# Order of ScalarE's work behind transform groups, and the steps in which first-stage groups run

## The chip, the cores and the metric

The kernel runs on one core of a Trainium2 chip. The metric is the device time of one execution in microseconds; lower is better. TensorE (PE) multiplies matrices and accumulates in PSUM banks of 128 partitions by 512 floats; VectorE (DVE), ScalarE (ACT) and GpSimd (POOL) work on elements; SyncE (SP) mostly issues DMAs. Each engine works through its own queue of instructions in the order in which the kernel wrote them.

## What is computed

The input x is 8 batches of 3008 tokens of 256 floats. First a Fourier transform along the tokens and one along the 256 features, of which the real part is kept; then a two-layer block with the quick gelu:

```
X = np.fft.fft(np.fft.fft(x, axis=1), axis=2).real.astype(np.float32)
h = X.reshape(24064, 256) @ w_in          # 256 x 2048
g = h * (1.0 / (1.0 + np.exp(-1.702 * h)))
out = g @ w_out                            # 2048 x 256
```

## The kernel before

**The transform.** The transform along the 3008 tokens is split as 47 by 64. For the next batch, b + 1, it is made while batch b goes through the two layers. `load_x` (L199) brings the batch to `xt` in SBUF, in four pieces; `fold1` (L210) adds and subtracts mirrored features on POOL, in 8 pairs of parts; `mix1` (L233) is the first stage: four groups of matmuls (m = 0 to 3) for each batch, each into two PSUM banks, `ps[0]` and `ps[1]`, that two ScalarE copies (L258) bring back to `xt`. Of the two copies, number r takes bank `ps[r]`. `spill` (L332) writes a finished group to DRAM (`Td`), and `fill` (L337) reads it back in another layout. `rotate` (L342) is a small correction of one column, and `stage2` (L349) is the second stage: 64 matmuls into two banks, and four DVE transposes of them to `pq`. The feature transform is folded into the first layer's weights (`wcs`). `paced` is a tiny DMA that holds back the DMAs behind it on SP's queue until a step's result is there.

**The steps.** The two layers run in 384 steps (L503): 8 batches x 3 blocks x 2 halves x 8 pairs of hidden groups. Step t makes two hidden groups of 128 for 256 tokens and their mirror tokens; in the second half of a batch's first block (steps 8 to 15 of its 48) a step is 226 tokens wide (`width`, L511). From step 8 on, the work of a step is this:

- `middle(t)` (L580): two ScalarE activations (L587) that write the rank-one term (the row `nb` times a weight per partition) to x's PSUM bank, `b0` or `b1` by the step's parity.
- `begin(t)` and `begin(t, 1)` (L590): 8 TensorE instructions each that add the even and then the odd part of the transform to that bank (rows "x<-pq,wcs" of the profile). A step starts with `begin(t, 1)` and issues `begin(t + 1)` later on.
- `doubled(t)` (L596, L599): ScalarE copies the bank, doubled, after `begin(t)` and before `begin(t, 1)` may add to it.
- `forward(t)` (L601): the gelu of the sum. `backward(t)` (L604, L560): a DVE subtraction that gives the mirror tokens, and `activate_back` (L609) their gelu.
- `sums` (L617 on POOL, L624 and L625 on DVE) and `deeper` (L646, DVE): sums for the second layer, which is multiplied by a seven-product scheme, one quarter of it once more in seven smaller ones.
- `product(t - 3)` (rows "o<-big,wo"), 12 instructions for most steps, and `small_products` (rows "low<-big", "o<-big,wo" of L680) of steps t - 3 and t - 4: the second layer, three steps behind (`LAG`). After 8 steps of one half the results are combined (`combine`, `combine_small`, `swap`, `combine_last`) and stored.

**The order.** It is written out by hand: the loop at L984 issues each step's work, and a table `extra` adds transform work at the end of chosen steps (`at`, L928; the loop that fills it for all batches is at L953). In a step that ends with `mix1` or `stage2` (`special`, L1022), x's bank of that parity and `b2` are lent to it, and `middle(t + 2)` is left out; the next step (`after`) makes up for it with `middle(t + 1)` ahead of `begin(t + 1)`. In an `after` step more of the products is placed ahead of `begin(t + 1)`. The order also changes in a step where the product three steps behind opens a new accumulation:

```
opening = (t - LAG) % NP == 0 and t >= NP + LAG
...
cut = 0 if opening and not after else 3 if after else 2
product(t - LAG, 0, cut)
...
    begin(t + 1)
...
product(t - LAG, cut, 6 if t - LAG == last else None)
```

`stage2` ends steps 8, 24 and 40 of a batch. `mix1` ended steps 12, 15, 19 and 23 of batches 1 to 6, and 16, 20, 25 and 28 of batch 0 (the last batch has none). `spill` follows in the step behind each group.

Of the kernel before, what the change touches and what calls it, by code (L numbers as in the profile page):

```python
# [50 lines left out]
def free(ap, offset, *dims):  # L51
    return bass.AP(ap.tensor, ap.offset + offset, [list(ap.ap[0])] + [list(d) for d in dims])
# [60 lines left out]
def kernel(ctx: ExitStack, tc, x, w_in, w_out, tab1, tab2, out):  # L113
    nc = tc.nc
    B, S, D = x.shape
# [53 lines left out]
    def bank(name, tag=None):  # L169
        if tag is None:  # L170
            tag = spare.pop(0)
            spare.append(tag)
        if tag in ("o0", "o1"):
            return o_banks[int(tag[1])]
        return (rest if tag[0] == "o" else psp).tile([128, 512], F32, tag=tag, name=name)
# [11 lines left out]
    xt = xp.tile([128, NJ, D], F32, tag="x", name="xt")  # L187
# [45 lines left out]
    def mix1(b, m):  # L233

        ps = [bank("ps1") for _ in range(2)]
        queues = {}
        for i in (2 * m, 2 * m + 1):
            for r in range(2):
                for c in range(2):
                    rows, o = slice(64 * r, 64 * r + NA), ps[r][64 * c:64 * c + 64, i % 2 * D:(i % 2 + 1) * D]  # L240
                    jj, todo = 4 * i + 2 * r + c, queues.setdefault((r, c), [])
                    if jj:
                        todo.append((2, o, mat(w1, jj, rows), xt[rows, 31 - (2 * i + c), :], not todo, True))
                        continue
                    for k, c0, c1 in ((0, 0, H + 1), (1, H + 1, D)):
                        for part in range(2):
                            todo.append((1, o[:, c0:c1], mat(w1, ENDS[k + 2 * part], rows), e0[b][:, part, c0:c1], not todo,
                                         part == 1))

        had = {key: 0 for key in queues}  # L250
        while any(queues.values()):
            key = min((key for key in queues if queues[key]), key=lambda key: (had[key], key))
            size, o, w, rhs, first, end = queues[key].pop(0)
            had[key] += size
            nc.tensor.matmul(o, lhsT=w, rhs=rhs, start=first, stop=end, skip_group_check=True)  # L255

        for r in range(2):
            nc.scalar.copy(free(xt[:], (4 * m + r) * D, [2 * D, 2], [1, D]), free(ps[r][:], 0, [D, 2], [1, D]))  # L258

# [314 lines left out]
    def activate(t):  # L576
        g = free(ht[t][:], 0, [256, 4], [1, width(t)])
        nc.scalar.activation(g, g, ACTF.Gelu_apprx_sigmoid)

    def middle(t):  # L580

        b, blk, hh, p = steps[t]
        n = width(t)
        x = xb[t] = bank("x", f"b{t % 2}")
        for i in range(2):
            f = 2 * p + i
            nc.scalar.activation(x[:, i * 256:i * 256 + n], nbt[b, blk][:, hh * 256:hh * 256 + n], ACTF.Copy,  # L587
                                 scale=af1[:, f:f + 1])
# [339 lines left out]
    def at(t, fn, *args):  # L928
        extra.setdefault(t, []).append((fn, args))

    n = len(steps)
# [20 lines left out]
        at(7 + i, small_weights, i)  # L952
    for b in range(B):  # L953
        t0 = b * NBLK * NF
        late = 0 if b else 5
        if b + 2 < B:
            for k in range(3):
                at(t0 + 11 + k, paced, t0 + 11 + k)
                at(t0 + 11 + k, turn, b + 2, k)
        if b + 1 < B:  # L960
            for c in range(NCH):
                for part in range(2):
                    at(t0 + 6 + 2 * c + part + late, fold1, b + 1, c, part, nc.gpsimd)
                if c % 2:
                    k = t0 + 9 + 2 * c + late + (c == (5 if late else 1))
                    at(k, mix1, b + 1, c // 2)
                    for half in range(2):
                        at(k + 1, spill, b + 1, half, c // 2)
            for blk in range(NBLK):
                at(t0 + 27 + blk + late, paced, t0 + 27 + blk + late)  # L970
                at(t0 + 27 + blk + late, fill, b + 1, 4 * blk, 4 * blk + 4)
            if b + 2 < B:
                for k in range(4):
                    at(t0 + 31 + 2 * k + late, paced, t0 + 31 + 2 * k + late)
                    at(t0 + 31 + 2 * k + late, load_x, b + 2, k)
            at(t0 + 36 + 3 * (late > 0), rotate, b + 1)
        for blk in range(NBLK):
            nxt = (b, blk + 1) if blk + 1 < NBLK else (b + 1, 0)
            if nxt[0] < B:
                at(t0 + blk * NF + 8, stage2, *nxt)  # L980
                at(t0 + blk * NF + 9, nyquist_out, *nxt)
                at(t0 + blk * NF + 10, nyquist, *nxt)

    for t in range(n + LAG):  # L984
        if t < NP:
            if t == NP - 3:
                spare[:] = [tag for tag in spare if tag[0] == "o"] + ["b2"]
            if t == NP - 1:
                middle(NP)
            hidden(t)  # L990
            if t == NP - 1:
                begin(NP)
                no_row(1024)
            if t == 0:
                squares(in2, nc.scalar)
                nyquist(0, 0)
                low_up(in2)
                low_down(in2)
            if t in rows_at:
                first_row(rows_at[t])  # L1000
            if t >= LAG and t != LAG + 1:
                product(t - LAG, 0, None)
            if t == LAG:
                product(1, 0, None)
            if t == 5:
                bounds(("out", 2))
            if t == 6:
                low_down(("out", 3))
            if t:
                activate(t - 1)  # L1010
            if t == 3:
                bounds(("in", 3))
            if t == 5:
                bounds(("out", 3), False)
            if t in early:
                fold_w(early[t])
            rows(t)
            if t == NP - 1:
                doubled(NP)
                middle(NP + 1)  # L1020
        else:
            after, special = (any(fn in (mix1, stage2) for fn, _ in extra.get(k, ())) for k in (t - 1, t))  # L1022
            if t < n:
                begin(t, 1)
            if t == NP:
                activate(t - 1)
            if t < n:
                forward(t)
            if after and t + 1 < n:
                middle(t + 1)  # L1030
            opening = (t - LAG) % NP == 0 and t >= NP + LAG
            one, other = (t - LAG, (1, 2, 4, 7)), (t - LAG - 1, (5, 6, 3))
            if opening:
                small_products(*other)
            cut = 0 if opening and not after else 3 if after else 2
            product(t - LAG, 0, cut)
            if after:
                small_products(one[0], one[1][:1])
                small_products(other[0], () if opening else other[1][:1])
            if t + 1 < n:  # L1040
                begin(t + 1)
            if not opening:
                small_products(other[0], other[1][after:])
            product(t - LAG, cut, 6 if t - LAG == last else None)
            small_products(one[0], one[1][after:])
            swap(t - LAG - 2)
            if t < n:
                backward(t)
            if t + 1 < n:
                doubled(t + 1)  # L1050
            if t < n:
                activate_back(t)
                sums(t, nc.gpsimd)
            if t + 2 < n and not special:
                middle(t + 2)
            combine_small(t - LAG - 1)
            if t - LAG == last:
                product(last, 6, None)
            sums(t - 1, nc.vector)
            deeper(t - 2, 0)  # L1060
            deeper(t - 3, 1)
        if t == NP:
            psu.close()
            low = ctx.enter_context(tc.tile_pool(name="low", bufs=1, space=PS))
            pot["low"] = low.tile([128, 3 * 512], F32, tag="low", name="low")
        if t >= LAG:
            combine(t - LAG)
            combine_last(t - LAG - 2)
            turn_last(t - LAG - 3, 0)
            turn_last(t - LAG - 4, 1)  # L1070
        if t >= NP:
            spare[:] = [f"b{t % 2}"] * special + ["b2"]
        for fn, args in extra.get(t, ()):
            fn(*args)
# [28 lines left out]
```

## Time and profile before

| | us |
|---|---|
| median of 3 runs | 1856.67 |
| lowest and highest run | 1856.37, 1859.4 |
| span of the profiled execution, first to last instruction | 1853.9 |
| TensorE busy in it | 1840.1 (99%) |
| VectorE busy | 1522.8 (82%) |
| ScalarE busy | 1145.5 (62%) |
| GpSimd busy | 972.4 (52%) |

The profile gives the profiled execution by its span alone; the runs' times lie 2.5 to 5.5 us above it. The profile is a record of every instruction of one execution: when it started, how long it took, and what ended the idle time of its engine before it. A matmul's duration covers its way through the array, in which the next one has long begun, so a busy TensorE can still have lost tenths of a microsecond between two groups of matmuls; the starts show it. "PEld" is the loading of weights, which runs ahead of the matmuls. The granted TensorE clock was 1.000 over the whole span.

### The profile page before, as it was taken

What the parts mean: (1) busy time and instruction counts of PE and PEld (TensorE: products, weight loads), DVE (VectorE), ACT (ScalarE), POOL (GpSimd) and SP (SyncE); (2) the same over time, 40 slices, a digit from 0 to 9 for tenths busy, and PEclk for the clock granted to TensorE, in tenths of its full rate; (3) what the DMA queues carried; (4) which work ended last, traced back from release to release, by engine and by line L of the source; (5) the groups of instructions that cost most, each with busy time, mean ns of one, the idle gap of its engine ahead of it and who ended that gap; (6) DMA issues with size and microseconds to landing.
All of it is one profiled execution on the core that took longest, in us unless ns stands there. A gap on an engine that the chain in (4) does not pass through costs nothing.

```text
span 1853.9 us, 56087 instructions
## 1 busy us (share of the span) xinstructions
PE 1840.1 (99%) x23722; PEld 1400.5 (76%) x23722; DVE 1522.8 (82%) x2222; ACT 1145.5 (62%) x2241; POOL 972.4 (52%) x1053
## 2 busy tenths in 40 slices
PE   8999999999999999999999999999999999999998
PEld 4677777777777777777777777777777777778776
DVE  6988778887798878987789878888888888878874
ACT  5656666665666566666665666666665666656563
POOL 4776436744367334773348634485445754434442
PEclk9999999999999999999999999999999999999999
DMA  8721341225011340223302142121411111100111
GB/s 277 184 61 34 85 68 19 72 52 99 19 46 48 77 77 13 52 50 90 57 13 69 41 86 52 20 74 34 103 33 21 37 46 36 31 19 13 23 19 24
DMA packets 149707, 105.31 MB, mean 57 GB/s; under 512 B 106057, under 2 KB 130665, under 8 KB 148896
## 3 DMA queue, kind: packets, MB, share of 16 engines
q1 hardware_dynamic: 146624, 99.68, 23.9%
q8 instruction: 187, 3.06, 0.7%
q10 hardware_dynamic: 2832, 2.05, 0.5%
q14 instruction: 64, 0.52, 0.1%
HBM read 64.41 MB, written 48.05 MB: 61 GB/s over the span
## 4 chain that ended last, share of the span: by engine, by line
PE 93%; DVE 2%; DMA 2%; POOL 1%; ACT 1%; issue 1%; DVEq 0%; SPq 0%; POOLq 0%; ACTq 0%
PE x L184 34%; PE o L184 26%; PE low L680 25%; PE o L680 4%; PE ps L255 2%; PE ps L360 1%; DVE big L646 1%; DMA xt<-in_x_dram 1%; DMA Td<-big 1%; ACT x L587 0%; DVE big L781 0%; PE po L184 0%; PE psw L184 0%; DMA big<-in_moe_w_in_dram 0%; DVE big L560 0%
## 5 line engine op out<-in xcount | busy, mean ns | idle before, releaser
L617 POOL TENSOR_TENSOR big<-big 128x256 f32<-128x256 f32 (+1 forms) x376 | 348.1, 926 | 829.1 <-ACT big L609 696.4
L184 PE MATMUL x<-pq,wcs 128*64 128x256 f32 (+1 forms) x6016 | 771.2, 377 | 1.1 <-ACT x L587 0.4
L646 DVE TENSOR_TENSOR big<-big 128x512 f32<-128x512 f32 (+1 forms) x736 | 625.6, 864 | 30.9 <-PE low L680 14.0
L184 PE MATMUL o<-big,wo 128*64 128x256 f32 (+1 forms) x4800 | 620.8, 375 | 0.0
L184 PEld LDWEIGHTS x<-pq,wcs 128*64 128x64 f32 x6016 | 409.8, 137 | 191.1 <-issue 15.0
L184 PEld LDWEIGHTS o<-big,wo 128*64 128x64 f32 x4800 | 341.7, 137 | 147.8 <-DVE big L624 0.5
L599 ACT ACTIVATE g<-x 128x512 f32<-128x512 f32 (+1 forms) x376 | 221.6, 589 | 374.7 <-PE x L184 373.5
L560 DVE TENSOR_TENSOR big<-g,x 128x512 f32<-128x512 f32 (+2 forms) x440 | 253.6, 588 | 196.6 <-ACT big L602 196.2
L680 PE MATMUL low<-big 128*64 128x128 f32 (+1 forms) x5888 | 382.8, 270 | 0.0
L587 ACT ACTIVATE x<-nb,af 128x256 f32<-128x256 f32 (+1 forms) x752 | 352.8, 469 | 12.2
L680 PEld LDWEIGHTS low<-big 128*64 128x64 f32 x5888 | 337.6, 137 | 29.2
L618 POOL TENSOR_TENSOR big<-big 128x256 f32<-128x256 f32 (+1 forms) x376 | 358.4, 953 | 0.0
L602 ACT ACTIVATE big<-x 128x512 f32<-128x512 f32 (+1 forms) x376 | 220.4, 586 | 195.9 <-PE x L184 159.8
L609 ACT ACTIVATE big<-big 128x512 f32<-128x512 f32 (+1 forms) x376 | 231.9, 617 | 41.1 <-DVE big L560 39.3
L680 PE MATMUL low<-big,wo 128*64 128x128 f32 (+1 forms) x2944 | 220.2, 270 | 0.1
L680 PEld LDWEIGHTS low<-big,wo 128*64 128x64 f32 x2944 | 171.6, 137 | 3.2 <-DVE big L646 0.4
L625 DVE TENSOR_TENSOR big<-big 128x512 f32<-128x512 f32 (+1 forms) x188 | 157.7, 839 | 6.5
L624 DVE TENSOR_TENSOR big<-big 128x512 f32<-128x512 f32 (+1 forms) x188 | 136.7, 727 | 5.4 <-POOL big L617 5.4
L781 DVE TENSOR_TENSOR big<-big,low 128x512 f32<-128x512 f32 (+3 forms) x184 | 109.0, 609 | 3.5
L680 PEld LDWEIGHTS o<-big,wo 128*64 128x64 f32 x1472 | 92.3, 137 | 24.9
L680 PE MATMUL o<-big,wo 128*64 128x128 f32 (+1 forms) x1472 | 110.0, 270 | 0.0
L227 POOL TENSOR_TENSOR xt<-xt 111x510 f32<-111x510 f32 x56 | 83.3, 1488 | 4.4
(95 smaller groups left out, 966.1 us busy)
## 6 DMA issues: line engine op xcount, KB each, us to landing
out_dram<-os SPq DMA_DIRECT2D x284, 64.0 KB
t<-Td SPq DMA_DIRECT2D x22, 512.0 KB
Td<-xt SPq DMA_DIRECT2D x56, 192.0 KB
xt<-in_x_dram SPq DMA_DIRECT2D x14, 512.0 KB
xt<-Xr SPq DMA_DIRECT2D x14, 512.0 KB
nb<-Nd SPq DMA_DIRECT2D x23, 256.0 KB
out_dram<-os SPq DMA_DIRECT2D x96, 56.0 KB
Xr<-in_x_dram SPq DMA_DIRECT2D x7, 752.0 KB
```

What stands on the lines that cost most here:

```text
L184: nc.tensor.matmul(out[c0:c0 + 64], lhsT=lhs[:, c0:c0 + 64], rhs=rhs, skip_group_check=True, **how)
L560: nc.vector.tensor_tensor(free(out, at + m - 1, [by, 2], [RUN, blocks], [-1, m]), *ins, op=op)
L587: nc.scalar.activation(x[:, i * 256:i * 256 + n], nbt[b, blk][:, hh * 256:hh * 256 + n], ACTF.Copy, scale=af1[:, f:f + 1])
L599: nc.scalar.activation(two(g[:], n), two(xb[t][:], n), ACTF.Copy, scale=2.0)
L602: nc.scalar.activation(front(t), two(xb[t][:], width(t)), ACTF.Gelu_apprx_sigmoid)
L609: nc.scalar.activation(back(t), back(t), ACTF.Gelu_apprx_sigmoid)
L617: eng.tensor_tensor(right(t, S1, n), left(t, A21, n), right(t, A22, n), op=ALU.add)
L618: eng.tensor_tensor(left(t, S3, n), left(t, A11, n), left(t, A21, n), op=ALU.subtract)
L624: eng.tensor_tensor(s2, s1, a11, op=ALU.subtract)
L625: eng.tensor_tensor(s4, a12, s2, op=ALU.subtract)
L646: nc.vector.tensor_tensor(out, i0, i1, op=how)
L680: nc.tensor.matmul(o, lhsT=lhs, rhs=rhs, start=first_in, stop=(p == NP - 2), skip_group_check=True)
```

## The change

Three things change. The rank-one term of the next step is issued to ScalarE ahead of the gelu in every step behind a first-stage or second-stage group. Of a first-stage group's two copies, the first stays where it was and the second goes behind that gelu, in the next step (a list `waiting` keeps it until then). And in batches 1 to 6 the groups end steps 16, 18, 21 and 26 of a batch; the folds, the fills and the loads of x that go with them are issued two steps later, and the rotation in step 39 for all batches. In batch 0 the steps are the same as before.

```diff
-        for r in range(2):
-            nc.scalar.copy(free(xt[:], (4 * m + r) * D, [2 * D, 2], [1, D]), free(ps[r][:], 0, [D, 2], [1, D]))
+        waiting.append((m, ps[1]))
+        mixed(m, 0, ps[0])
+
+    waiting = []
+
+    def mixed(m, r, ps):
+        nc.scalar.copy(free(xt[:], (4 * m + r) * D, [2 * D, 2], [1, D]), free(ps[:], 0, [D, 2], [1, D]))
...
-        late = 0 if b else 5
+        late = 2 if b else 5
+        mixes = (16, 18, 21, 26) if b else (16, 20, 25, 28)
...
                 for part in range(2):
                     at(t0 + 6 + 2 * c + part + late, fold1, b + 1, c, part, nc.gpsimd)
                 if c % 2:
-                    k = t0 + 9 + 2 * c + late + (c == (5 if late else 1))
+                    k = t0 + mixes[c // 2]
                     at(k, mix1, b + 1, c // 2)
...
                     at(t0 + 31 + 2 * k + late, load_x, b + 2, k)
-            at(t0 + 36 + 3 * (late > 0), rotate, b + 1)
+            at(t0 + 39, rotate, b + 1)
...
+            if after and t + 1 < n:
+                middle(t + 1)
             if t < n:
                 forward(t)
-            if after and t + 1 < n:
-                middle(t + 1)
+            while waiting:
+                m, ps = waiting.pop()
+                mixed(m, 1, ps)
             opening = (t - LAG) % NP == 0 and t >= NP + LAG
```

## The prediction

> **What bounds the kernel now.** I write "step 13" for step 13 of a batch's 48. First the page: the sums by engine and the chain that ended last.
>
> ```profile
> span 1853.9 us, 56087 instructions
> ...
> PE 1840.1 (99%) x23722; PEld 1400.5 (76%) x23722; DVE 1522.8 (82%) x2222; ACT 1145.5 (62%) x2241; POOL 972.4 (52%) x1053
> ...
> PE 93%; DVE 2%; DMA 2%; POOL 1%; ACT 1%; issue 1%; DVEq 0%; SPq 0%; POOLq 0%; ACTq 0%
> ```
>
> TensorE (PE) is the bound: whatever makes it wait lengthens the kernel, and work elsewhere costs nothing until PE waits for it. 99% hides waits of tenths, because a matmul's modelled end covers them. So I measured whole steps, from the start of a step's first group of 8 matmuls into x (`begin(t, 1)`) to the next one's, in the timeline, and had busy times by such windows. Steps 12 to 15 of batch 1, 226 wide, with first-stage groups at the end of 12 and 15 (columns: window, length, then busy PE, PEld, DVE, ACT, POOL with counts):
>
> ```profile
> 325.89:331.65 5.76, 5.76 (x84) 4.57 (x80) 5.69 (x10) 4.47 (x9) 4.81 (x6) 1.00 0.67 217
> 331.65:335.90 4.25, 4.21 (x53) 3.18 (x52) 4.15 (x7) 2.92 (x7) 3.70 (x4) 1.00 0.14 47
> 335.90:340.17 4.27, 4.27 (x62) 3.61 (x62) 4.13 (x8) 3.29 (x8) 3.78 (x5) 1.00 0.19 34
> 340.17:345.23 5.06, 5.06 (x73) 3.55 (x69) 4.96 (x8) 1.92 (x4) 4.22 (x6) 1.00 0.53 121
> sum 19.34, PE 19.30 PEld 14.90 DVE 18.93 ACT 12.60 POOL 16.50; mean PE 4.83 PEld 3.73 DVE 4.73 ACT 3.15 POOL 4.13
> ```
>
> VectorE (DVE) is busy 18.93 of 19.34: these steps have no room on it. The same four steps of the last batch, which has no groups and no folds:
>
> ```profile
> 1682.74:1687.36 4.62, 4.44 (x63) 3.47 (x61) 4.48 (x10) 3.31 (x7) 2.19 (x3) 1.00 0.09 18
> ...
> sum 16.60, PE 16.42 PEld 13.37 DVE 16.18 ACT 11.91 POOL 8.02; mean PE 4.10 PEld 3.34 DVE 4.05 ACT 2.98 POOL 2.00
> ```
>
> Step 14 lasts 4.62 there, against 4.22 in the first batch. The timeline says why:
>
> ```profile
> 1682.44 0.68 DVE L560 TENSOR_TENSOR big<-g,x 128x448 f32<-128x448 f32 x2
> ...
> 1683.15 0.58 ACT L609 ACTIVATE big<-big 128x452 f32<-128x452 f32 x1 [1.13 <-DVE big L560]
> ...
> 1683.64 0.92 ACT L587 ACTIVATE x<-nb,af 128x226 f32<-128x226 f32 x2
> ...
> 1684.62 0.60 PE L184 MATMUL x<-pq,wcs 128*64 128x226 f32 x4 [0.18 <-ACT x L587]
> ```
>
> `backward` of step 13 ends 0.38 after step 14 began, the gelu and the rank-one pair (L587) queue behind it on ScalarE (ACT), and PE starts x at 1684.62 instead of 1684.27 (two groups of 0.76 after 1682.74): 0.35 late.
>
> The wait that the new order removes, in step 13 of batch 1, and then (step 25) the wait that two group places get:
>
> ```profile
> 333.20 0.95 ACT L587 ACTIVATE x<-nb,af 128x226 f32<-128x226 f32 x2
> ...
> 334.20 0.58 PEld L184 LDWEIGHTS x<-pq,wcs 128*64 128x64 f32 x8 [0.26 <-ACT x L587]
> ```
>
> ```profile
> 392.13 1.08 PE L184 MATMUL x<-pq,wcs 128*64 128x256 f32 x8
> ...
> 393.05 0.61 PE L680 MATMUL low<-big 128*64 128x128 f32 x8
> 393.32 0.60 ACT L599 ACTIVATE g<-x 128x512 f32<-128x512 f32 x1 [1.25 <-PE x L184]
> ...
> 393.49 0.61 PE L680 MATMUL low<-big,wo 128*64 128x128 f32 x8
> ...
> 393.98 0.44 PE L184 MATMUL x<-pq,wcs 128*64 128x256 f32 x2
> ```
>
> `begin(t+1)` (392.13) must end, L599 (`doubled`) must copy it, and only then may `begin(t+1, 1)` (393.98) add to the bank. Start to start is 1.85; 16 small matmuls cover 0.87 of it.
>
> **The change, part by part.**
>
> *Rank-one before the gelu, second copy after it.* No instruction is added. Steps behind a group in batch 1, against the same step without one (last batch; step 14: first batch): 13: 4.25 to 3.83; 14: 4.27 to 4.22; 16: 4.73 to 4.42; 20: 5.07 to 4.77; 21: 4.39 to 4.33; 24: 6.07 to 5.95. Together 1.26. The first x group behind a group takes 1.08 instead of 1.03 even though nothing is late there (345.23), and I let that stay, 4 x 0.05. So 1.06 goes per batch. Behind a second-stage group: step 25 4.51 against 4.33 (step 27), of which 0.05 stays and 0.06 is L599's wait above, gives 0.07; step 41 (4.55) 0.12; step 9 0.03: together 0.22 (ends 0 and 0.34). The pair now waits ahead of the gelu for two transposes (389.58 to about 390.4) and ends near 391.4, before PE wants it at 391.7; the gelu and the DVE subtraction behind it start 0.8 later, into 0.58 of DVE idle in that step and 1.47 in the next, at no cost. The second copy (0.59) ends near 2.8 into the step, and ACT's next work, L599, begins at 3.85: hidden. Its bank is next asked for two steps later at the earliest.
>
> *Groups to steps 16, 18, 21, 26, from 12, 15, 19, 23 (batches 1 to 6).* The matmuls and copies are the same, so their own time moves along. What differs is the step behind each:
> - 19 and 27 are steps in which the oldest product opens an accumulation (t - 3 divisible by 8), as no step behind a group or second stage was before. In that branch the loop puts all small products and all twelve product matmuls ahead of `begin(t+1)`, and nothing behind it: `begin(t+1, 1)` follows at once. Without cover PE idles 1.85 - 0.92 = 0.93, and the next x group starts cold, 0.05 to 0.06 more: 0.99 each, 1.98 per batch (ends 1.86 and 1.98).
> - 17: behind `begin(18)` stand 16 narrow small matmuls, 0.77, against the 0.93: 0.16, and 0.05 for the restart: 0.21. 22 has 24 small ones behind it, 1.31: nothing.
>
> *Narrow steps lose their groups.* Steps 12 and 13 then last 4.22 + 3.83 = 8.05. In batch 1 `backward` of step 13 ends at 334.90, 9.01 after step 12 began, at the end of a DVE queue with hardly a gap. With the same queue it is 0.96 late, and by the last batch's 0.38 to 0.35 PE loses 0.93 in step 14, and 0.05. For step 15 it ended 17.45 after; the steps would then end at 17.2: 0.2 more. That makes 1.2 by batch 1's rows and 0.40 by the last batch's, whose DVE shares nothing with folds. I take 1.0, nearer to batch 1, whose folds stay; high end 1.5.
>
> *Folds two steps later.* The extra-row work of the first fold (0.72 + 0.59 + 0.72 on POOL, by the first batch's rows at 102.93) falls in step 9, where DVE is busy 4.22 of 4.22: 0 to 0.4, I take 0.1. The last folds reach step 24; the first batch, whose folds run late too, has 4.66 for 4.33 in step 23 and 6.10 for 6.07 in 24: 0 to 0.36, I take 0.2. The Trainium skill, "SBUF — State Buffer", section "Who interferes with whom", has a rule against this part: a DVE instruction with two SBUF inputs and a GpSimd one that reads SBUF exclude each other for an instruction's whole length. Here POOL has 16.50 - 8.02 = 8.48 more in the four narrow steps than in the last batch, DVE only 18.93 - 16.18 = 2.75; by the rule's worst reading the rest, 5.7 per batch, would be added to the sum, an estimate of about 1903; the rows pass on a third, and I go by them.
>
> *Queues.* On SP the spills go out at steps 17, 19, 22, 27 (before 13, 16, 20, 24), fills at 29 to 31, loads of x at 33 to 39, each two later; the last spill stands two steps (some 9 us) ahead of the first fill instead of three. The load-to-fold distance is unchanged. The rotation goes from step 36 to 39, where the first batch had it: 36 and 37 cost 0.09 and 0.03 over 4.77 and 4.33, 39 and 40 of the first batch 0.09 and 0.03. Nothing; without cover a late fill would show as a wait at the rotation.
>
> *Sum*, per batch 1 to 6: -1.06 - 0.22 + 1.98 + 0.21 + 1.0 + 0.1 + 0.2 = +2.21, six times 13.3. Batch 0 has only the new order (its groups stay at 16, 20, 25, 28, none ahead of an opening): step 17 0.21, 21 0.06, 25, 26 and 29 0.15, 9 and 41 0.3: -0.7. Step 12 of batch 6 was 6.39 instead of 5.76: -0.6. Last batch -0.1. Net +11.9: a span of 1865.8 from 1853.9, and, the 2.8 between span and the runs' median of 1856.67 kept, 1868.6. Low: 1.86, second-stage gain 0.34, narrow 0.4, no fold cost, 1861.7; high: no second-stage gain, 1.5, 0.4 and 0.36, 1876.
>
> **The rivals.**
> - *Narrow steps absorb everything*: DVE loses its backlog, since steps 16 and 17 leave it 4.73 - 2.61 and 4.03 - 2.32 idle. Against it: the last batch stalls even without folds. 0.91 per batch, total +4.1: 1860.8.
> - *The two openings are covered* (not slower). If PE didn't have to wait for L599 there, the +1.98 falls away and the rest, 0.23 x 6 - 1.4, is nothing: 1856.7; with the narrow steps also free, 1849. For it: no step of the trace shows this order. Against it: step 25's 0.06 wait on the same copy. It decides below 0.33 per opening.
> - *DVE and POOL fall behind further* in the shortened narrow steps, 2.4 instead of 1.0: 1877. For it: POOL's 16.50 in what will be 16.2; against it, the stall itself gives both time.
>
> **How the numbers follow.** Forecast 0.64; first rival 0.16; openings covered 0.10, half of it with narrow steps free; further behind 0.10. About 0.2% (3.7 us) can be told from no change. Slower: 0.64 + 0.10 + 0.11 of the first rival = 0.85; same 0.05 + 0.05; faster 0.05. The range 1859 to 1877 leaves out the covered openings and about half of the last rival and some of the first.
>
> **What would show it.** Steps 19 and 27 of batches 1 to 6 with about 0.93 between L599's x group and the next, and L599's row as what ended it; no wait of x on L587 in steps 17, 19, 22 and 27; step 14 near 5.2 and waiting on L587 behind L560; 12, 13, 15 near 4.2, 3.8, 3.9; DVE busy all through them. Wrong if openings show other matmuls there, or step 14 stays near 4.2.

## The result and the profile after

The changed kernel takes 1869.73 us in the median (1867.64 to 1870.85), the kernel before 1856.67 (1856.37 to 1859.4): a ratio of 1.0066, 95% interval 1.0056 to 1.0077. It is slower by 13.1 us, where +11.9 was forecast. The profiled execution has a span of 1867.3. Lines of the old kernel stand 5 further down in the new one, so L560 is now L565, L587 is L592 and L599 is L604.

The page of the changed kernel, its sums by engine and its chain:

```profile
span 1867.3 us, 56094 instructions
...
PE 1839.1 (98%) x23722; PEld 1400.4 (75%) x23722; DVE 1519.0 (81%) x2222; ACT 1149.9 (62%) x2241; POOL 977.3 (52%) x1053
...
PE 84%; DVE 12%; ACT 2%; DMA 2%; issue 1%; DVEq 0%; POOL 0%; ACTq 0%; SPq 0%; POOLq 0%
```

PE is as busy as before (1839.1 against 1840.1) and the span is 13.4 longer: PE has no more work, it waits more. In the chain DVE has grown from 2% to 12%. That does not mean that DVE became the bound of the whole kernel; it means that at some places the chain now runs back through a stretch of DVE's queue. PE's own waits in the changed kernel say at which places (engine, tile and line that waited, what ended the wait: us in total, times, longest):

```profile
PE x L184 <- ACT g L604: 9.1, 12, 0.8
PE x L184 <- ACT x L592: 4.8, 7, 0.8
PE warm L335 <- DVE wcs L851: 2.7, 1, 2.7
PE psw L184 <- DMA small<-in_tab_dram: 1.9, 1, 1.9
PE ps L255 <- DVE big L565: 1.5, 7, 0.2
```

The third and fourth are of the start. The other three are what the change made, but for a wait of 0.17 on L592 in the last batch, which was there before. Twelve waits of 0.8 on `doubled` (L604) are two in each of six batches. Of the seven waits on the rank-one pair (L592) six are in step 14 of batches 1 to 6, and of the seven of a first-stage group for its bank (L565) six are at the end of step 16. Before, the same view had a single wait of a first-stage group for L560, 0.5 long, and two of x for L587, 0.4 together.

Windows give the places. These are steps 12 to 15 of batch 1 in the changed kernel with their sum, then steps 16, 17, 19 and 27 (window, length, busy PE, PEld, DVE, ACT, POOL):

```profile
326.26:330.48 4.22, 4.22 (x63) 3.56 (x61) 4.18 (x8) 3.99 (x9) 3.83 (x4) 1.00 0.63 184
330.48:334.31 3.83, 3.83 (x57) 3.17 (x55) 3.69 (x5) 2.29 (x5) 3.19 (x4) 1.00 0.49 167
334.31:339.51 5.20, 4.43 (x62) 3.46 (x60) 5.10 (x10) 2.39 (x5) 5.04 (x5) 1.00 0.01 3
339.51:343.52 4.01, 4.01 (x57) 3.09 (x55) 3.98 (x8) 3.02 (x7) 3.32 (x5) 1.00 0.44 76
sum 17.26, PE 16.49 PEld 13.28 DVE 16.95 ACT 11.69 POOL 15.37; mean PE 4.12 PEld 3.32 DVE 4.24 ACT 2.92 POOL 3.84
...
343.52:349.80 6.28, 6.05 (x85) 4.59 (x81) 6.14 (x7) 2.72 (x6) 4.46 (x6) 1.00 0.23 45
349.80:354.04 4.24, 4.24 (x54) 3.18 (x53) 2.63 (x5) 3.19 (x7) 2.78 (x4) 1.00 0.18 37
359.63:364.79 5.16, 4.40 (x56) 3.08 (x53) 3.24 (x7) 3.18 (x7) 1.96 (x4) 1.00 0.26 71
400.55:405.86 5.31, 4.56 (x56) 3.23 (x52) 2.92 (x6) 3.18 (x7) 0.00 (x0) 1.00 0.28 63
```

Steps 19 and 27 have 0.76 and 0.75 of visible PE idle, and so has step 14, whose neighbours 12, 13 and 15 are as short as the forecast had them. DVE is busy 16.95 of the 17.26 in the four narrow steps. The timeline of the changed kernel at these places: the opening in step 19, the narrow step 14, and the end of step 16 (start, duration, engine, line, operation; in brackets the idle time before it and what ended that):

```profile
334.60 0.68 DVE L565 TENSOR_TENSOR big<-g,x 128x448 f32<-128x448 f32 x2
...
335.80 0.92 ACT L592 ACTIVATE x<-nb,af 128x226 f32<-128x226 f32 x2
...
336.77 0.98 PE L184 MATMUL x<-pq,wcs 128*64 128x226 f32 x8 [0.77 <-ACT x L592]
...
342.88 4.79 DVE L651 TENSOR_TENSOR big<-big 128x452 f32<-128x452 f32 x3
...
347.60 0.68 DVE L565 TENSOR_TENSOR big<-g,x 128x512 f32<-128x512 f32 x1
...
348.33 0.32 PE L255 MATMUL ps<-e,w 47*64 47x129 f32 x1 [0.23 <-DVE big L565]
...
363.00 1.03 PE L184 MATMUL x<-pq,wcs 128*64 128x256 f32 x8
364.14 0.60 ACT L604 ACTIVATE g<-x 128x512 f32<-128x512 f32 x1 [1.76 <-PE x L184]
...
364.79 1.08 PE L184 MATMUL x<-pq,wcs 128*64 128x256 f32 x8 [0.76 <-ACT g L604]
```

In the opening PE has nothing between the two x groups: the first ends at 364.03, the copy runs from 364.14 to 364.74, the next group starts at 364.79. In step 14 the subtraction of step 13 ends 0.97 after step 14 began; the gelu of the mirror tokens waits for it, and the rank-one pair stands behind that gelu on ScalarE. At the end of step 16 the group waits for a bank that a late subtraction (347.60) still reads; on DVE it stands behind three sums of `deeper` (L651) that took 4.79.

Step by step over the whole trace, from start of step to start of step. The first four rows set a step of the changed kernel beside the same step without the cost that is meant, from the kernel that is named; the last two are after minus before:

| steps of a batch | us per batch |
|---|---|
| 19 and 27 (5.16 and 5.31 against 4.23 and 4.38 in the third experiment, with cover); 20 and 28, behind them (4.82 against 4.77) | +0.93, +0.93; +0.05, +0.05 |
| 14 (5.21 against 4.22 in the first batch), 15 (4.00 against 3.93 there) | +0.99, +0.07 |
| 16 (6.28 against 5.96 in the first batch) | +0.32 |
| 17 (4.24 against 4.03 in the last batch) | +0.21 |
| whole batch 1, 2, 3, 5 (batch 4) | +2.29 (+2.22) |
| batch 0, batch 6, batch 7 | -0.71, +1.71, -0.14 |

The batches add up to +12.2. The last 1.1 of the span's 13.4 lies ahead of step 8 (it began at 80.80 before and at 81.91 after), where the program is the same; over all profiled kernels here, that start lay between 80.1 and 82.2, so I count it as scatter and not as an effect of the change.

### The profile page after: what moved, and what is told of

It is laid out like the page before. It is cut to its first block, busy times and chain, and to the rows that moved or that the text cites. A ratio compares the mean times of both kernels' runs of the same rounds, so it can differ in the third digit from the quotient of the medians.

```text
span 1867.3 us, 56094 instructions
## 1 busy us (share of the span) xinstructions
PE 1839.1 (98%) x23722; PEld 1400.4 (75%) x23722; DVE 1519.0 (81%) x2222; ACT 1149.9 (62%) x2241; POOL 977.3 (52%) x1053
## 4 chain that ended last, share of the span: by engine, by line
PE 84%; DVE 12%; ACT 2%; DMA 2%; issue 1%; DVEq 0%; POOL 0%; ACTq 0%; SPq 0%; POOLq 0%
PE x L184 30%; PE o L184 23%; PE low L685 22%; DVE big L651 5%; PE o L685 4%; DVE big L565 2%; PE ps L255 2%; PE ps L365 1%; DVE big L786 1%; DVE big L629 1%; DMA xt<-in_x_dram 1%; ACT g L604 1%; DMA big<-in_moe_w_out_dram 1%; DVE os L737 1%; DVE big L630 0%
## 5 line engine op out<-in xcount | busy, mean ns | idle before, releaser
L622 POOL TENSOR_TENSOR big<-big 128x256 f32<-128x256 f32 (+1 forms) x376 | 356.5, 948 | 836.2 <-ACT big L614 728.1
L651 DVE TENSOR_TENSOR big<-big 128x512 f32<-128x512 f32 (+1 forms) x736 | 641.9, 887 | 23.4 <-PE low L685 4.6
L604 ACT ACTIVATE g<-x 128x512 f32<-128x512 f32 (+1 forms) x376 | 221.7, 590 | 370.8 <-PE x L184 369.6
L565 DVE TENSOR_TENSOR big<-g,x 128x512 f32<-128x512 f32 (+2 forms) x440 | 254.5, 590 | 223.7 <-ACT big L607 223.5
L592 ACT ACTIVATE x<-nb,af 128x256 f32<-128x256 f32 (+1 forms) x752 | 352.8, 469 | 82.9 <-DVE pq L371 48.2
L623 POOL TENSOR_TENSOR big<-big 128x256 f32<-128x256 f32 (+1 forms) x376 | 363.5, 967 | 0.0
L630 DVE TENSOR_TENSOR big<-big 128x512 f32<-128x512 f32 (+1 forms) x188 | 139.5, 742 | 6.5
```

Of the source, the lines that this page charges most:

```text
L565: nc.vector.tensor_tensor(free(out, at + m - 1, [by, 2], [RUN, blocks], [-1, m]), *ins, op=op)
L604: nc.scalar.activation(two(g[:], n), two(xb[t][:], n), ACTF.Copy, scale=2.0)
L622: eng.tensor_tensor(right(t, S1, n), left(t, A21, n), right(t, A22, n), op=ALU.add)
L623: eng.tensor_tensor(left(t, S3, n), left(t, A11, n), left(t, A21, n), op=ALU.subtract)
L630: eng.tensor_tensor(s4, a12, s2, op=ALU.subtract)
L651: nc.vector.tensor_tensor(out, i0, i1, op=how)
```

## The experiments

Three things had to be told apart: what the new order on ScalarE is worth without the new places; whether the openings really cost because nothing covers `doubled`; and whether the stall of the narrow steps is DVE's, slowed by the folds, or something of the new order. Each ratio is to the kernel before, run on the same chip, with its 95% interval. A difference from the changed kernel is one between medians of separate series, in which the kernel before itself lay between 1855.82 and 1856.67; so such differences are also given by the steps of the two traces, from the start of step 8 on.

### The order alone

The groups go back to where they were; ScalarE's order stays changed.

```diff
-        late = 2 if b else 5
-        mixes = (16, 18, 21, 26) if b else (16, 20, 25, 28)
+        late = 0 if b else 5
...
-                    k = t0 + mixes[c // 2]
+                    k = t0 + 9 + 2 * c + late + (c == (5 if late else 1))
...
-            at(t0 + 39, rotate, b + 1)
+            at(t0 + 36 + 3 * (late > 0), rotate, b + 1)
```

> Only the new order on ScalarE; groups, folds, fills, loads and rotation in the steps of before. Theory (the order helps, the places cost): step 13 about 4.05, 16 about 4.47, 25 and 41 about 4.44; the swap's copies still hold step 20 near 5.0; some 0.8 us per batch go in batches 1 to 6 and 0.7 in batch 0, so about 1851 us. Rival (the order itself costs, since the gelu and the subtraction behind it start later): slower than 1856.7, with longer steps behind groups.

Measured: 1855.42, ratio 0.9995 (0.9985 to 1.0004): no gain, a miss. The steps that were to gain did: 13 went from 4.25 to 3.99, 16 from 4.74 to 4.47, 25 and 41 to 4.44. But step 11 went from 3.98 to 4.15, step 12 from 5.76 to 6.39, and step 20 from 5.08 to 5.23. The timeline of this kernel, steps 9 and 10 and the end of step 12 of batch 1, and at last one row of step 10 of batch 5:

```profile
315.15 0.94 ACT L592 ACTIVATE x<-nb,af 128x226 f32<-128x226 f32 x2 [3.47 <-DVE pq L371]
...
316.03 0.53 ACT L607 ACTIVATE big<-x 128x452 f32<-128x452 f32 x1
...
316.59 0.69 DVE L565 TENSOR_TENSOR big<-g,x 128x448 f32<-128x448 f32 x2 [0.89 <-ACT big L607]
...
320.82 1.11 POOL L231 TENSOR_TENSOR xt<-xt 111x254 f32<-111x254 f32 x1
...
321.38 2.29 DVE L630 TENSOR_TENSOR big<-big 128x452 f32<-128x452 f32 x1
...
321.89 0.66 POOL L622 TENSOR_TENSOR big<-big 128x226 f32<-128x226 f32 x1
...
322.51 0.67 POOL L623 TENSOR_TENSOR big<-big 128x226 f32<-128x226 f32 x1
...
323.14 0.59 POOL L225 TENSOR_TENSOR xt<-xt 111x4 f32<-111x4 f32 x1
...
330.79 0.68 DVE L565 TENSOR_TENSOR big<-g,x 128x448 f32<-128x448 f32 x2
...
331.61 0.29 PE L255 MATMUL ps<-e,w 47*64 47x129 f32 x1 [0.51 <-DVE big L565]
...
1221.17 1.04 DVE L630 TENSOR_TENSOR big<-big 128x452 f32<-128x452 f32 x1
```

Behind the second stage of step 8 ScalarE now waits for two transposes (3.47 idle), then makes the rank-one pair, and only then the gelu that DVE's subtraction needs. DVE stands idle for 0.89 in step 9. That alone costs nothing: before, DVE had 0.74 idle ahead of the subtraction of step 10, this idle time is now used up, and that subtraction ends 6.6 after step 9 began in both kernels. What is late is behind it. The sum L630 of step 10 took 2.29 instead of the 1.04 of the kernel before, beside three POOL instructions that ran meanwhile, and DVE has hardly a gap from there to step 12. So the subtraction of step 12 ends 17.7 after step 9 began instead of 16.9, and the first-stage group at its end waits for its bank. Batch 5 of the same execution tells the two apart: DVE is idle for 0.89 in step 9 there too, but the sum took 1.04 (1221.17), and steps 11 and 12 lasted 3.98 and 5.76 as before. In the five other batches the 0.8 of steps 11 and 12, with the 0.15 of step 20, cancels what the order gains elsewhere.

### The new places alone

The order on ScalarE goes back; the groups stay in steps 16, 18, 21 and 26.

```diff
-        waiting.append((m, ps[1]))
-        mixed(m, 0, ps[0])
+        for r in range(2):
+            nc.scalar.copy(free(xt[:], (4 * m + r) * D, [2 * D, 2], [1, D]), free(ps[r][:], 0, [D, 2], [1, D]))
...
-            if after and t + 1 < n:
-                middle(t + 1)
             if t < n:
                 forward(t)
-            while waiting:
-                m, ps = waiting.pop()
-                mixed(m, 1, ps)
+            if after and t + 1 < n:
+                middle(t + 1)
```

> Only the new places; rank-one pair behind the gelu and both copies ahead of it, as before. Theory: steps 14, 16, 19 and 27 lengthen as in the changed kernel, and the waits for the rank-one pair that the order removes stay (17 near 4.5, 22 near 4.85, 25 near 4.51, 41 near 4.55), so slower than the changed kernel, about 1873 us. Rival (the order costs): not slower than the changed kernel's 1869.7.

Measured: 1873.15, 1.0088 (1.0073 to 1.0103). As expected: 17.3 over the kernel before. The same waits are there without the new order:

```profile
PE x L184 <- ACT g L599: 9.1, 12, 0.8
PE x L184 <- ACT x L587: 5.0, 8, 0.8
```

So the loss belongs to the places. At these places the new order gives back 1873.15 - 1869.73 = 3.4 us by the medians, and 5.2 by the steps.

### Openings with cover

In an opening step behind a group the products go behind `begin(t + 1)`, as in other openings.

```diff
-            cut = 0 if opening and not after else 3 if after else 2
+            cut = 0 if opening else 3 if after else 2
```

> The changed kernel, but in a step that is both behind a group and an opening the twelve product instructions stay behind the next step's first half, where the other openings have them. Theory (TensorE has nothing to do there while the doubled copy is made): steps 19 and 27 of batches 1 to 6 go from 5.16 and 5.31 to about 4.2 and 4.35; 12 x 0.98 less, about 1858 us. Rival (ScalarE is late there because the second copy stands behind the gelu): the wait moves but stays, 1869 us.

Measured: 1863.53, 1.0038 (1.0023 to 1.0053). Both openings became as short as expected (19: 5.16 to 4.23, 27: 5.31 to 4.38), which shows the mechanism: once twelve product matmuls stand between the two x groups, the 0.8 waits on `doubled` are gone. But the kernel won 6.2 us over the changed kernel (5.0 by the steps), where it was to win 11. This kernel's waits of PE, its steps 19 and 21, and the end of step 21:

```profile
PE ps L255 <- DVE big L565: 5.8, 12, 0.7
PE x L184 <- ACT x L592: 4.8, 7, 0.8
```

```profile
357.84:362.07 4.23, 4.23 (x56) 3.22 (x54) 2.35 (x5) 3.54 (x7) 1.99 (x4) 1.00 0.16 33
366.84:373.26 6.42, 5.68 (x73) 3.61 (x69) 6.28 (x9) 3.22 (x6) 5.15 (x5) 1.00 0.00 0
```

```profile
371.50 0.68 DVE L565 TENSOR_TENSOR big<-g,x 128x512 f32<-128x512 f32 x1
...
372.23 1.09 PE L255 MATMUL ps<-xt,w 47*64 47x256 f32 x16 [0.74 <-DVE big L565]
```

L604 is no longer in the list. In its place the group at the end of step 21 waits 0.74 for the bank that the subtraction reads, and step 21 lasts 6.42 instead of 5.46: DVE is busy 6.28 of it. In the changed kernel DVE had used the 0.93 that TensorE waited in step 19 to work off its queue; the sixth experiment tests this. With step 30 (4.77 to 4.91) that gives back 1.1 of the 1.96 per batch that steps 19, 20, 27 and 28 won.

### Both copies ahead of the gelu

```diff
-        waiting.append((m, ps[1]))
         mixed(m, 0, ps[0])
+        mixed(m, 1, ps[1])
```

> The changed kernel, but both copies follow their group at once, ahead of the rank-one pair and the gelu. Theory (ScalarE is idle for 0.9 us ahead of the doubled copy, so the place of the second copy costs nothing): within 1 us of 1869.7; only step 17, whose rank-one pair would end near 2.3, close to the 2.45 at which TensorE wants it, might wait. Rival (the second copy matters): steps 17 and 22 longer by up to 0.5, 6 us in all, or, if its new place is what delays the doubled copy at the openings, 11 us less.

Measured: 1870.53, 1.0073 (1.0058 to 1.0088), which is 0.8 above the changed kernel and inside the spread of both. The runs cannot tell the two; by the steps of the traces this kernel is 2.1 longer, so the place of the second copy is not quite free. Step 21 went from 5.46 to 5.74 in each of the six batches: the group at its end now waits 0.2 for its bank (L565). Why that subtraction is later was not tried. Beside it a single step is 0.1 to 0.3 longer in each of three batches; step 17 stayed. Of the 5.2 by which the order shortened the second experiment's kernel, the rank-one pair's place thus makes 3.1 and the second copy's 2.1.

### No folds in batches 1 to 6

```diff
+        if b > 1:
+            return
         at, up = 2 * c * D, (31 - 2 * c) * D
```

> The changed kernel, but the folds of batches 2 to 7 are left out (only their extra row is made), so the first stage works on unfolded data there. Theory (the narrow steps stall because VectorE, slowed by the folds beside it, frees x's bank late): step 14 of batches 1 to 6 falls from 5.21 to the 4.62 of the last batch, 15 from 4.00 to 3.93, 16 from 6.28 to about 5.97; 19 and 27 stay at 5.16 and 5.31; about 6 us less than 1869.7, so 1864. Rival (the narrow steps stall because TensorE's shorter steps leave ScalarE too little time, whatever VectorE does): 14 and 16 as they were, 1869.7.

Measured: 1862.61, 1.0036 (1.0022 to 1.0049), as expected. This kernel's waits of PE, its steps 14 and 16 of batch 1, and the three sums ahead of the subtraction of step 16 (its lines stand 2 further down than in the changed kernel):

```profile
PE x L184 <- ACT g L606: 9.1, 12, 0.8
...
PE x L184 <- ACT x L594: 1.5, 7, 0.5
```

```profile
332.93:337.52 4.59, 4.43 (x62) 3.46 (x60) 4.45 (x10) 3.30 (x7) 2.18 (x3) 1.00 0.10 18
341.46:347.42 5.96, 5.96 (x84) 4.57 (x81) 2.82 (x5) 2.36 (x5) 3.08 (x4) 1.00 0.18 36
```

```profile
339.92 1.97 DVE L653 TENSOR_TENSOR big<-big 128x452 f32<-128x452 f32 x3
```

The openings' waits are unchanged to the last digit, while step 14 falls from 5.20 to 4.59, nearly the 4.62 that it has in the last batch of the kernel before, and the bank wait of step 16 is gone (6.28 to 5.96). POOL has 2.18 in step 14 instead of 5.04, DVE 4.45 instead of 5.10 with the same ten instructions, and the three sums took 1.97 instead of 4.79. The narrow stall and step 16's wait are therefore made by a DVE that works beside the folds, and about 0.4 of step 14 is there without them. That rest is not one fixed size: in the last batch, which has folds in neither kernel, step 14 is 4.95 here and 4.61 in the changed kernel, and no run shows why.

### Cover and no folds together

The edits of the last and of the third experiment together.

> The kernel with covered openings, with the same folds left out. Theory (what step 19 won was taken back in step 21, where the group waits for the bank that a late VectorE subtraction frees): step 21 falls from 6.41 to 5.46 and 30 from 4.91 to 4.77, 19 and 27 stay at 4.23 and 4.38, and 14 to 16 as without folds; 2.05 per batch, 12 us less than 1863.5, about 1851. Rival (the wait in step 21 comes with the changed order of the products): 21 stays near 6.4, and 1857.

Measured: 1851.68, 0.9977 (0.9968 to 0.9986), as expected. Step 19 is 4.23, step 27 is 4.38, step 30 is 4.85, halfway to the 4.77 that was expected, and step 21 no longer gives it back:

```profile
367.88:373.37 5.49, 5.49 (x72) 3.70 (x68) 5.39 (x7) 2.72 (x6) 2.58 (x3) 1.00 0.00 0
```

Cover alone won 6.2, no folds alone 7.1, both 18.1 (by the steps 5.0, 5.6 and 16.3). The two terms are not additive: the cover is only worth its 11 where DVE has no queue to work off. The ratio itself says little about the change, since the kernel before has its folds in.

### The order, but not in step 9

From here on each edit is shown against an earlier experiment. This one is the first experiment, with the gelu ahead of the rank-one pair in step 9 alone, where it delayed DVE.

```diff
-            if after and t + 1 < n:
+            last_pair = t % 48 == 9
+            if after and t + 1 < n and not last_pair:
                 middle(t + 1)
             if t < n:
                 forward(t)
+            if after and t + 1 < n and last_pair:
+                middle(t + 1)
```

> Only the new order, in the places of before, but in step 9, which is narrow and behind the second stage, the gelu goes first again as before. Theory (the rank-one pair's wait for the transposes put off the gelu, and with it VectorE's subtraction, by 0.9 in a stretch where VectorE never catches up, and step 12's group then waited for its bank): step 11 back from 4.17 to 3.98 and 12 from 6.39 to 5.76, about 0.8 us per batch, 1851 us. Rival (steps 11 and 12 were late for the sake of the order behind the first-stage groups): they stay, 1855.4.

Measured: 1851.33, 0.9972 (0.9962 to 0.9983), as expected. Step 11 is 3.98 again and step 12 is 5.76. Putting step 9 alone back won 4.1 us over the first experiment (4.0 by the steps), so the delay of that one gelu had cost what the order won. It did so by another way than the expectation says: DVE does catch up in step 10, and what is gone is the long sum, which takes 1.04 again in step 10 of all six batches. The kernel is faster than both kernels of this case; 0.6 of that is batch 6, whose step 12 was 6.39 in the kernel before.

### The second copy later still

The last experiment, with the second copy behind the mirror tokens' gelu in every step.

```diff
-            while waiting:
-                m, ps = waiting.pop()
-                mixed(m, 1, ps)
             opening = (t - LAG) % NP == 0 and t >= NP + LAG
...
                 sums(t, nc.gpsimd)
+            while waiting:
+                m, ps = waiting.pop()
+                mixed(m, 1, ps)
             if t + 2 < n and not special:
```

> As the kernel with the gelu first in step 9, and the second copy goes behind the gelu of the mirror tokens, so behind the doubled copy too. Theory (in step 20 the three copies of the swap, the second copy, the rank-one pair and the gelu all stand ahead of the doubled copy, and TensorE waits 0.4 for it): step 20 falls from 5.23 to about 4.85, 0.35 x 6 less, about 1849 us. Rival (the swap alone is late): 20 stays near 5.2.

Measured: 1854.83, 0.9995 (0.9986 to 1.0004): a miss, 3.5 above the last. Step 20 fell to 4.82 as expected. But 24 rose from 6.01 to 6.50, and the second step behind each of the other groups lost a little (14: 4.27 to 4.53, 17: 4.03 to 4.11, 21: 4.38 to 4.60); there the rank-one pair that the loop issues next now queues behind the copy, which I take for the reason without having tried it by itself. The end of step 24 in the timeline of this kernel:

```profile
387.62 0.58 ACT L263 COPY xt<-ps 128x512 f32<-128x512 f32 x1
387.74 1.65 PE L365 MATMUL ps<-t,small 64*32 64x128 f32 x64
...
388.24 0.87 PEld L365 LDWEIGHTS ps<-t,small 64*32 64x32 f32 x62 [0.38 <-ACT xt L263]
```

The second stage starts into its first bank and then needs the one that the copy (L263) is still emptying: its 64 matmuls take 1.65 instead of 1.16. Here a group (step 23) and the second stage (24) lie only one step apart.

### The third group in step 21

The seventh experiment with the groups in steps 12, 15, 21 and 23, which keeps step 20 free of a group's copies in the step that also swaps results.

```diff
-                    k = t0 + 9 + 2 * c + late + (c == (5 if late else 1))
+                    k = t0 + ((12, 15, 21, 23) if b else (16, 20, 25, 28))[c // 2]
```

> The kernel with the new order but for step 9, and its third group at the end of step 21 instead of 19 (batches 1 to 6), so that no group's successor holds the swap's copies. Theory (step 20 waits 0.4 because the swap shares ScalarE with the work behind a group, and VectorE, busy for almost all of 18 to 23, allows little less than before): step 20 falls to about 4.8, step 21 lasts 5.5 to 5.9 since its group waits for a bank from a late VectorE, and the batch is 0 to 0.4 us shorter: 1849 to 1851.5. Rival (VectorE is the bound of the whole stretch): no gain or a loss, 1851.5 or more.

Measured: 1850.13, 0.9973 (0.9962 to 0.9984), within what was expected; by steps it wins 0.16 per batch over the seventh (19 is 4.18, 20 is 4.77, 21 is 5.74). The medians, 1.2 apart, can hardly tell the two.

### The second copy behind the swap only

The seventh experiment, with the second copy later in step 20 of a batch alone, where it stood between the swap's copies and `doubled`.

```diff
-            while waiting:
+            while waiting and t % 8 != 4:
                 m, ps = waiting.pop()
                 mixed(m, 1, ps)
...
                 sums(t, nc.gpsimd)
+            while waiting:
+                m, ps = waiting.pop()
+                mixed(m, 1, ps)
```

> The kernel with the new order but for step 9, and only in steps that hold the swap's copies does the second copy go behind the gelu of the mirror tokens. Theory (the second copy cost step 24 its bank and steps 14 and 17 their rank-one pair when it went last everywhere; in step 20 alone it frees the doubled copy): 14, 17 and 24 back at 4.27, 4.03 and 6.01, 20 at 4.82 instead of 5.22, 21 at 4.60 instead of 4.38: 0.2 per batch, about 1850 us. Rival (the gain of 20 is given back in 21 and behind it in full): 1851.3 or more.

Measured: 1849.65 (1849.27 to 1850.04) against 1856.05, ratio 0.9966 (0.9952 to 0.9979), as expected, and the fastest of all. Its page and its waits of PE:

```profile
span 1847.5 us, 56093 instructions
...
PE 92%; ACT 3%; DVE 2%; DMA 2%; issue 0%; SPq 0%; POOL 0%; DVEq 0%; ACTq 0%; POOLq 0%
```

```profile
PE x L184 <- ACT x L592: 0.3, 2, 0.2
PE ps L255 <- DVE big L565: 0.2, 1, 0.2
```

DVE's share of the chain is 2% again, and of the waits that the changed kernel had 0.5 us are left of 15.4. The order of the change is a gain of 0.34% at the old places, once step 9 and step 20 are excepted.

## Why the prediction was right

**Openings.** 1.98 per batch was forecast, 1.96 measured: 0.93 in each of steps 19 and 27, and 0.05 for the restart in each of the steps behind them. That is as worked out from the start-to-start of the old step 25 and the matmuls that were not there to cover it. The start-to-start itself is 1.79 here (363.00 to 364.79) and not 1.85; the step it was read from had an x group that was itself restarted, and the same 0.05 to 0.06 stood in the 0.92 that was taken off. The third experiment shows the cause, the twelve waits on L604 in the list.

**Step 17.** 0.21 forecast, 0.21 measured in the step, though put together differently: 0.05 of it is the slower x group behind a group, which the forecast carried in the 4 x 0.05 that it let stay, and the restart behind the wait falls into step 18. Step 22, forecast at nothing but its share of that 4 x 0.05, has 0.05.

**Rank-one pair and second stage.** -1.06 and -0.22 were forecast. Steps 13 and 20 went to 3.83 and 4.82 (forecast 3.83 and 4.77), steps 9, 25 and 41 gained 0.19 together, and no x group behind a moved group waits for L592. The sum came out, but the forecast gave all of the 1.06 to the order, and that is too much: without the order, at the new places, the second experiment's batches are only 0.63 to 0.89 longer, 0.26 of it in steps 9, 25 and 41. So the order itself took 0.4 to 0.6 of the 1.06; the rest went because the groups left their old steps. Batch 0, which has only this part, gained 0.71 for the 0.7 forecast, though not quite where it was forecast: 17 gained 0.27, and 23 lost 0.07.

**Narrow steps.** Forecast 1.0, measured 0.99 in step 14, 0.07 in 15 and 0.32 in 16, together about 1.4: this term was mis-sized. The subtraction of step 13 ended 9.02 after step 12 began, against 9.01 assumed, and made step 14 what batch 1's rows gave (0.93 and 0.05). Choosing 1.0 between 0.40 and 1.2 was too low, since step 14 alone took it. And the second stall has another place: the forecast gave 0.2 to step 15, whose x group would follow late, but it came at the end of step 16, where the group needs the bank that the late subtraction reads. That group had not been there before, and its own wait was not among the prediction's steps.

**Folds in steps 9, 23 and 24.** 0.3 was forecast, nothing was measured: 9 is 4.19 (before 4.21), and steps 23 and 24, with 4.33 and 5.96, are at the times of steps without folds. This too-high term offset most of the narrow steps' too-low one: that the sum came so close is in part luck. The worst reading of the rule of exclusion between DVE and POOL, which the prediction weighed and set aside, would have made 1903; the time shows nothing like it, though single DVE instructions did stand still beside POOL (last section).

**"0.8 later ... at no cost."** True for steps 25 and 41, which DVE's idle time covers. It was said of the second stage in general, and in step 9 it holds for the delay itself, which DVE's idle time in step 10 takes up. But the delay also shifts DVE's instructions against POOL's. In the changed kernel, whose folds come two steps later, that was free; at the old places it made one sum 1.25 longer in five of six batches, which cost about 0.8 in each of them (the first and seventh experiments).

**The rivals.** That the narrow steps absorb everything fell with step 14 at 5.21. That the openings are covered fell with steps 19 and 27; and its price was wrong too. It took 1.98 per batch away and left the other terms, 1856.7. The kernel with covered openings takes 1863.5, because the openings' idle time had been DVE's time to catch up (1.1 of the 1.96 per batch came back). DVE and POOL falling further behind is what happened in part, 1.4 between the forecast's 1.0 and that rival's 2.4; the fifth and sixth experiments show that the folds are behind it.

**The sum.** By batches 2.29 against 2.21, 12.2 in all against 11.9. Not forecast is the 1.1 that this execution's start came later.

## What to carry to other kernels

A wait of the bound engine is priced by what its queue holds between the two ends of the wait: read the dependent pair's start-to-start from any step, subtract the work that the new place leaves between them, and the result here was right to 0.01. A stretch with a near-full second engine has its room in the bound engine's own work: taking work out of it, or taking away an idle gap behind it, brings that engine's queue forward as a new wait, so each removed stall has to be priced again with the next engine's backlog. The same reordering can be free in one step and cost as much as its whole delay in another; look at every step in which it occurs for the engine that feeds on the delayed result, and not only for that engine's idle time: a shift can also bring two of its neighbours' instructions together that slow each other.

## What the runs showed of the hardware

A DVE sum beside POOL can stand still for several POOL instructions. In step 10 of the first experiment (rows at 320.82 to 323.14) the sum L630 took 2.29. The same sum, of the same shape, took 0.63 in step 12. While it was under way, two POOL instructions of 128x226 ran from start to end in 0.66 and 0.67, as short as this shape ever is in that trace. The POOL instruction behind them, under way when the sum ended, took 0.59, where the same line had taken 0.21 in step 9. So the sum did not share with POOL: its record holds more than a microsecond in which POOL worked at full speed, and POOL's record of 0.59 holds time in which it stood still in turn. In other rows the two take turns one by one, and both are longer, as in step 10 of batch 5, where the sum took 1.04 and a POOL instruction of 128x226 beside it 1.05. The Trainium skill, "SBUF — State Buffer", section "Who interferes with whom", says that a DVE instruction with two SBUF inputs contends with a GpSimd one that reads SBUF, under an exclusive lock. These rows agree with it. What it costs over a stretch is less than POOL's added time: in step 14, between the changed kernel and the one without folds, 2.86 more of POOL (5.04 against 2.18) cost DVE 0.65 (5.10 against 4.45) for the same ten instructions, and a part of the 2.86 can itself be time that POOL stood still.

PE's modelled ends hide a part of each wait: step 19 has 0.76 of idle in the windows and lost 0.93 by the wait, step 14 0.77 and 0.94. The rest, 0.17, stands in the trace as busy time of the last matmuls ahead of the wait. The x group behind a wait then takes 1.08 instead of 1.03, or 0.98 instead of 0.93 in a narrow step, which makes the restart of 0.05. The granted clock stayed at 1.00 in all these steps.
